# GLU weight gradients: where the attention weights' pieces stand, where the last tile's hh is read from, and when dA's last columns are fetched

## The chip, the cores and the metric

The kernel runs as one program on one core of a Trainium2 chip. The core has five engines that run side by side, each with its own instruction stream in a fixed order: TensorE (PE; its weight loads are listed as PEld), VectorE (DVE), ScalarE (ACT), GpSimd (POOL) and SyncE (SP). Data moves between the device memory (DRAM) and the core's memory (SBUF) by DMA; SP, ACT and POOL issue transfers, each on a queue of its own (q1 is SP's, q10 ACT's, q0 POOL's), and all of them share 16 DMA engines. TensorE writes into PSUM, from which DVE or ACT "evacuates" a result to SBUF.

The metric is the time of one launch in microseconds (us). Three runs of the kernel before gave 3058.02, 3062.4 and 3064.0, median 3062.4.

## The reference, cut to what matters

The program computes the output and all gradients of a two-part layer: a segmented attention with a memory (64 segments of 32 rows, 32 heads of 128) and a gated linear unit (GLU), for 2048 rows of width 512 and a hidden width of F = 1792:

```python
def _B_ref(x, w_gate, w_up, w_down):
    g = jnp.einsum('bsd,df->bsf', x, w_gate)
    u = jnp.einsum('bsd,df->bsf', x, w_up)
    h = _sigmoid(g) * u
    return jnp.einsum('bsf,fd->bsd', h, w_down)
...
x = x + ga * _A_ref(h, A_mem0, A_Wq, A_Wk, A_Wv, A_Wo, A_seg_len)
h = _layernorm(x, axis=-1) * (1 + cb) + sb
x = x + gb * _B_ref(h, B_w_gate, B_w_up, B_w_down)
```

The change lies in the backward pass of the GLU. With h2 the GLU's input rows, hh = sigmoid(g) * u, db the gradient at the GLU's output, and dg and du the gradients at g and u, the three weight gradients are sums over all 2048 rows:

- dW_down = hh^T db (1792 x 512, output 9),
- dW_gate = h2^T dg and dW_up = h2^T du (512 x 1792 each, outputs 7 and 8).

## The kernel before

The program runs in phases. Phase 2 is the attention forward, phase 3 the GLU forward and backward with its weight gradients, phase 4 the attention backward, phase 5 the attention's weight gradients. The change is in phase 3 and in what is prepared there for phase 4.

**The GLU's tiles.** The 2048 rows go through as NT = 16 tiles of 128 rows in a pipeline of seven stages, `s0` to `s6`, one step per iteration `it`, the deepest stage first (`run_pipeline`, L1373). `s2` makes g and u with w_gate and w_up and, in a late part, hh (L1213), which POOL stores to HHROWS (L1214). `s3` makes du and dg (L1232 to L1238); SP turns hh around with a transposing DMA (L1225). `s4` multiplies by w_down (L1247) and turns du and dg around, duT (L1250) and dgT (L1251). `s5` makes the gradient at the GLU's input from duT and dgT (L1272). `s6` sums over rows (L1315), transposes da, the gradient for the attention's output (L1319), and SP stores it to DAOT (L1323). hh, du, dg and the rest live in the pool `sbp`; hh has two buffers.

**W_down's gradient.** Once the last tile has left `s2`, the space of w_gate and w_up (`Wk`) is free. `dbr` (all 2048 rows of db, 2 MB) is loaded there by ACT (L1355, at it = NT + 1) and `hr_0` (all 16 tiles of hh's first 384 columns) by SP (`load_hr(0)`, L1339, at it = NT + 2). hh's other columns come in groups `hr_1` to `hr_4` of 384 columns (the last has 256) into a ring of two places in `Wv`. `wd_chunk(fc)` (L1341 to L1347) makes 128 rows of dW_down: 16 products, one per tile, summed in one PSUM bank, then an evacuation, by ACT and DVE in turns, and a store by POOL. Chunks 0 to 2 (out of hr_0) run inside the pipeline's last steps; chunks 3 to 13 follow in the block with the pools `p3g_o` and `p3g_ps`.

**W_gate's and W_up's gradients.** After that come 2 x NCH = 8 column chunks (4 for dg, 4 for du) of CH = 448 columns, each with DC = 4 results of 128 rows, each result again 16 products (L1427). dg's or du's chunk of columns is loaded by ACT as `xr` (`load_xr`, L1403, 1792 KB) into the same ring of two places in `Wv`, two chunks ahead, and h2 as `h2r` (L1415, 2 MB). The first, `load_xr(0)`, is issued after W_down's chunk 11, when hr_3 has been read.

**The attention weights' pieces.** Phase 4 needs the attention's four weight matrices transposed (WoT, WvT, WkT, WqT). This is cut into 32 pieces (`p4_weights_setup_pieces`, L1468 on): each loads 512 KB by SP into one of three places (`stage0`, `stage1` and a part of `Wv`; L1488 and L1502), runs 16 transposes on TensorE (L1493 and L1506) into two PSUM banks, and has four evacuations by DVE and ACT. `emit_setup()` (L1395) spreads them over the 19 steps of the block, 11 chunks of dW_down and 8 column chunks.

**dA's last columns.** Phase 4 begins with the last four segments. `get_db(15)` (L1464) has SP load the last tile of DAOT (`daq`, L1459) and POOL copy from it (`dyb`, L1466). It is called after W_down's chunk 4.

The order of instructions on each engine is made when the program is built: a scheduler places what the source emits, by readiness, and `pin` fixes parts of it. `evac` is a helper, so evacuations have its lines (L61 for ACT, L63 for DVE).

Of the kernel before, what the change touches and what calls it, by code (L numbers as in the profile page):

```python
# [40 lines left out]
class K:  # L41
# [1035 lines left out]
    def phase3(self):  # L1077
        nc, tc, cfg, io = self.nc, self.tc, self.cfg, self.io
        D, DC, F, FC, NT, T = cfg.D, cfg.DC, cfg.F, cfg.FC, cfg.NT, cfg.T
        CH = 448  # L1080
        NCH = F // CH
# [5 lines left out]
        with ExitStack() as ctx:  # L1087
# [16 lines left out]
            def mm():  # L1104
                return psM.tile([128, 512], F32, name="mm", tag="m")
# [88 lines left out]
            def s2(j, st):  # L1194
                r0, r1 = j * 128, (j + 1) * 128
                hdT = st["hdT"]
                sg = sbp.tile([128, F], BF16, name="sg", bufs=2)
                u = sbp.tile([128, F], BF16, name="u", bufs=1)
                hh = sbp.tile([128, F], BF16, name="hh", bufs=2)
                umh = sbp.tile([128, F], BF16, name="umh", bufs=1)  # L1200
                for ch in range(NCH):
                    sl = slice(ch * CH, (ch + 1) * CH)
                    gp = mm()
                    for c in range(DC):
                        nc.tensor.matmul(gp[:, 0:CH], lhsT=hdT[:, c, :], rhs=w_gate[:, c, sl], start=(c == 0), stop=(c == DC - 1))
                    nc.scalar.activation(sg[:, sl], gp[:, 0:CH], AF.Sigmoid)
                    up = mm()
                    for c in range(DC):
                        nc.tensor.matmul(up[:, 0:CH], lhsT=hdT[:, c, :], rhs=w_up[:, c, sl], start=(c == 0), stop=(c == DC - 1))
                    self.evac("act", u[:, sl], up[:, 0:CH])  # L1210

                def out():
                    nc.vector.tensor_tensor(hh[:], sg[:], u[:], op=ALU.mult)  # L1213
                    nc.gpsimd.dma_start(self.HHROWS[r0:r1, :], hh[:])  # L1214
                    nc.vector.tensor_tensor(umh[:], u[:], hh[:], op=ALU.subtract)

                late.append(out)
                st.update(sg=sg, hh=hh, umh=umh)
                return st

            def s3(j, st):
# [107 lines left out]
            dbr = self.flat(self.Wk, 0, NT * D).rearrange("p (j d) -> p j d", j=NT)  # L1329
            hr_0 = self.flat(self.Wk, NT * D, NT * 384).rearrange("p (j f) -> p j f", j=NT)  # L1330
            hrs = {0: hr_0}
# [3 lines left out]
            kk = [0]  # L1335

            def load_hr(g):
                w = min(384, F - 384 * g)
                (nc.sync if g < 2 else nc.scalar).dma_start(hrs[g][:, :, 0:w], self.HHROWS[:, 384 * g:384 * g + w].rearrange("(j p) f -> p j f", p=128))  # L1339

            def wd_chunk(fc, ps, ot):  # L1341
                for j in range(NT):
                    nc.tensor.matmul(ps[:], lhsT=hrs[fc // 3][:, j, (fc % 3) * 128:(fc % 3) * 128 + 128], rhs=dbr[:, j, :],
                                     start=(j == 0), stop=(j == NT - 1))
                self.evac("act" if kk[0] % 2 == 0 else "dve", ot[:], ps[:])
                kk[0] += 1
                nc.gpsimd.dma_start(io["out_9"][fc * 128:(fc + 1) * 128, :], ot[:])  # L1347

            def after(it):
                for f in turns.pop(it, []):  # L1350
                    f()
                if it == 2:
                    self.pin(i0, [ET.PE, ET.Activation])
                if it == NT + 1:
                    nc.scalar.dma_start(dbr, self.DBROWS[:, :].rearrange("(j p) d -> p j d", p=128))  # L1355
                elif it == NT + 2:
                    load_hr(0)
                elif NT + 3 <= it < NT + 6:
                    if it == NT + 3:
                        load_hr(1)  # L1360
                    wd_chunk(it - NT - 3, mm(), sbp.tile([128, D], BF16, name="ot2", tag="db", bufs=2))
# [4 lines left out]
            def after(it):  # L1366
# [3 lines left out]
                if it >= 5:  # L1370
                    later(it)

            self.run_pipeline(NT, [s0, s1, s2, s3, s4, s5, s6], deepest_first=True, after=after)  # L1373
            self.pin(i0, [ET.DVE])
            self.pin_behind(i0, self.pinned, [ET.PE, ET.DVE, ET.Activation, ET.Pool, ET.SP])
# [8 lines left out]
        with ExitStack() as ctx:  # L1384
            op_ = ctx.enter_context(tc.tile_pool(name="p3g_o", bufs=2, reuse_waits="tile"))
            psG = ctx.enter_context(tc.tile_pool(name="p3g_ps", bufs=4, space=PSUM, reuse_waits="tile"))
            setup_pieces = self.p4_weights_setup_pieces(ctx)
            n_chunks = 2 * NCH + FC - 3
            n_setup, done = len(setup_pieces), [0]

            def emit_setup():
                done[0] += 1
                while setup_pieces and (n_setup - len(setup_pieces)) * n_chunks < done[0] * n_setup:
                    setup_pieces.pop(0)()
            h2r = self.flat(self.Wk, NT * D, NT * D).rearrange("p (j d) -> p j d", j=NT)  # L1395
            load_hr(2)
            xrs = []

            def load_xr(i):
                if i < 2 * NCH:  # L1400
                    rows, ch = ((self.DGROWS, self.DUROWS)[i // NCH], i % NCH)
                    t = ring[i % 2].rearrange("p (j f) -> p j f", j=NT)
                    nc.scalar.dma_start(t, rows[:, ch * CH:(ch + 1) * CH].rearrange("(j p) f -> p j f", p=128))  # L1403
                    xrs.append(t)

            for fc in range(3, FC):
                wd_chunk(fc, psG.tile([128, D], F32, name="gps2", tag="g"), op_.tile([128, D], BF16, name="ot2", tag="o"))
                if fc == 4:
                    self.get_db(cfg.NS // 4 - 1)
                if fc == 5:  # L1410
                    load_hr(3)
                elif fc == 8:
                    load_hr(4)
                elif fc == 9:
                    nc.scalar.dma_start(h2r, self.H2ROWS[:, :].rearrange("(j p) d -> p j d", p=128))  # L1415
                elif fc == 11:
                    load_xr(0)
                emit_setup()
            load_xr(1)
            k = kk[0]  # L1420
            for (rows, outw) in ((self.DGROWS, io["out_7"]), (self.DUROWS, io["out_8"])):
                for ch in range(NCH):
                    xr = xrs.pop(0)
                    for c in range(DC):
                        ps = psG.tile([128, CH], F32, name="gps", tag="g")
                        for j in range(NT):
                            nc.tensor.matmul(ps[:], lhsT=h2r[:, j, c * 128:(c + 1) * 128], rhs=xr[:, j, :],  # L1427
                                             start=(j == 0), stop=(j == NT - 1))
                        ot = op_.tile([128, CH], BF16, name="ot", tag="o")
                        self.evac("act" if k % 2 == 0 else "dve", ot[:], ps[:])  # L1430
                        k += 1
                        nc.gpsimd.dma_start(outw[c * 128:(c + 1) * 128, ch * CH:(ch + 1) * CH], ot[:])
                    load_xr(NCH * (outw is io["out_8"]) + ch + 2)
                    emit_setup()
            while setup_pieces:
                setup_pieces.pop(0)()
        self.wvk_ctx.close()
# [852 lines left out]
```

## Time and profile before

| | us |
|---|---|
| profiled execution | 3064.78 |
| its span | 3063.0 |
| median of the three timed runs | 3062.4 |
| mean granted TensorE clock | 0.991 |
| last product of the GLU's tiles before W_down's chunk 0 (L1247) ends | about 1295.4 |
| W_down's chunk 0 starts | 1299.63 |
| W_down's chunk 3 starts | 1319.27 |
| W_gate's first product starts | 1391.62 |
| last product of W_up ends | about 1503.6 |
| phase 4's first product with dOst (L1742) starts | 1519.57 |

Times inside the execution count from the start of the span. The profile lists, for each engine, its instructions with start and duration; a bracket after a row says how long the engine was idle before it and what it then waited for. A row of several like instructions gives the start of the first and the duration of all of them. A view of stretches gives, for each stretch, the busy time of the engines, the clock that TensorE was granted (1.00 is full) and the share and rate of the DMA engines.

### The profile page before, as it was taken

The page shows a single profiled execution, that of the slowest core. Times are in us where ns is not written, and L with a number is a line of the kernel's source. Part 1 is how long each engine was busy: PE and PEld are TensorE (multiplying, and loading weights), DVE is VectorE, ACT ScalarE, POOL GpSimd, SP SyncE. Part 2 cuts the span into 40 slices and gives each one's busy share as a digit, 9 for nine tenths or more (in the row PEclk, how much of TensorE's full clock was granted, in tenths as well). Part 3 has the DMA queues.
Part 4 walks back from the last instruction along what each step waited for, and adds up shares of the span by engine and source line. Part 5 has one row for each costly group of instructions (what it writes and reads, how often), then busy time and mean ns, then how long its engine had stood idle before and what let it go on. Part 6 is the DMA issues. An engine that isn't in the chain of part 4 may idle for free. (4 is left out here: it accounts for less than half of the span.)

```text
span 3063.0 us, 106593 instructions
## 1 busy us (share of the span) xinstructions
PE 2975.5 (97%) x44297; PEld 1859.8 (61%) x44297; DVE 1605.9 (52%) x3744; ACT 1288.2 (42%) x3182; POOL 1220.6 (40%) x2645
## 2 busy tenths in 40 slices
PE   6999999999998999989899999999999999999999
PEld 3666666666665544445567777777777754445454
DVE  5566566656656788732255555555555632322230
ACT  2555565555554533321255555555555520101011
POOL 2555555555554222211344444444444422333321
PEclk8999999999999999999999999999999999999999
DMA  9888888888888899987499999999999997666574
GB/s 307 217 219 209 216 220 205 219 215 210 217 215 265 199 230 229 239 254 246 155 248 248 245 246 243 247 246 253 248 239 248 246 284 265 214 193 220 182 247 140
DMA packets 838567, 703.54 MB, mean 230 GB/s; under 512 B 538722, under 2 KB 711042, under 8 KB 837188
## 3 DMA queue, kind: packets, MB, share of 16 engines
q1 hardware_dynamic: 712916, 486.69, 64.3%
q0 software_dynamic: 54512, 148.63, 15.3%
q10 hardware_dynamic: 70656, 61.41, 6.4%
q8 instruction: 348, 5.70, 0.8%
q14 instruction: 135, 1.11, 0.1%
HBM read 295.19 MB, written 276.35 MB: 187 GB/s over the span
## 5 line engine op out<-in xcount | busy, mean ns | idle before, releaser
L2080 PE MATMUL gps<-rows,hrows 128*128 128x512 bf16 (+2 forms) x2160 | 417.5, 355 | 0.0
L2080 PEld LDWEIGHTS <-hrows 128*128 128x128 bf16 x2160 | 211.3, 98 | 204.5
L63 DVE CAST ot<-gps 128x512 bf16<-128x512 f32 (+3 forms) x76 | 48.2, 634 | 294.7 <-PE gps L2080 208.4
L1786 POOL COPY dOst<-RAd 96x512 bf16<-96x512 bf16 x128 | 75.1, 611 | 307.6 <-DVE RAd L63 307.3
L61 ACT ACTIVATE ot<-gps 128x512 bf16<-128x512 f32 (+3 forms) x75 | 41.3, 551 | 359.9 <-PE gps L2080 214.7
L658 PE MATMUL pass_ps<-Wv,hT 128*32 128x512 bf16 (+2 forms) x2304 | 188.2, 357 | 0.0
L2084 POOL DMA_DIRECT2D out_dram<-ot x108 | 81.4, 753 | 260.3 <-DVE ot L63 132.7
L1034 POOL TENSOR_TENSOR Pst<-Pst,rden 120x1408 bf16<-120x1408 bf16 x63 | 159.8, 2536 | 56.7 <-issue 35.3
L255 PEld LDWEIGHTS <-hT 128*32 128x32 bf16 x4096 | 125.1, 97 | 94.2 <-DMA Wq<-in_A_Wq_dram 4.6
L61 ACT ACTIVATE dVT<-g_ps 128x480 bf16<-128x480 f32 (+1 forms) x192 | 104.7, 545 | 97.8 <-PE g_ps L1742 97.4
L63 DVE CAST Vst<-pass_ps 96x512 bf16<-96x512 f32 x128 | 87.3, 682 | 106.4 <-ACT RBv L61 101.3
L215 PE MATMUL dh_ps<-WvT,dVT 128*32 128x512 bf16 x2048 | 134.3, 382 | 0.1
L2094 PE MATMUL gps5o<-WoT,rows 128*128 128x512 bf16 x592 | 128.4, 379 | 1.8 <-DMA rows<-OSR 1.8
L255 PE MATMUL pass_ps<-Wq,hT 128*32 128x512 bf16 x2048 | 125.6, 383 | 4.5 <-DMA Wq<-in_A_Wq_dram 4.5
L223 PE MATMUL at_ps<-Wo,OT 128*32 128x256 bf16 x4096 | 124.6, 274 | 2.8 <-DMA Wo<-in_A_Wo_dram 2.4
L658 PE MATMUL pass_ps<-Wv,hb 128*32 128x512 bf16 (+2 forms) x636 | 127.2, 345 | 0.0
L255 PE MATMUL pass_ps<-Wk,hT 128*32 128x512 bf16 x2048 | 124.8, 381 | 1.8 <-POOL hT L547 1.1
L255 PE MATMUL pass_ps<-WoT,dyT 128*32 128x256 bf16 (+1 forms) x3072 | 122.7, 308 | 0.9 <-ACT dyT L1860 0.9
L223 PE MATMUL dhq_ps<-WqT,dQT 128*32 128x256 bf16 x4096 | 122.9, 273 | 0.0
L793 POOL DMA_DIRECT2D Vst<-RBv x192 | 99.2, 522 | 58.6 <-ACT ET L840 38.3
L215 PE MATMUL dh_ps<-WkT,dKT 128*32 128x512 bf16 x2048 | 122.3, 380 | 0.0
L223 PEld LDWEIGHTS <-dQT 128*32 128x32 bf16 x4096 | 109.8, 97 | 15.6
(448 smaller groups left out, 7007.5 us busy)
## 6 DMA issues: line engine op xcount, KB each, us to landing
OSR<-Ost SPq DMA_DIRECT2D x64, 352.0 KB
OT<-OT SPq DMA_DIRECT2D x64, 352.0 KB
VT<-VTr SPq DMA_DIRECT2D x64, 352.0 KB
PS<-Pst SPq DMA_DIRECT2D x64, 352.0 KB
OT_l<-OT SPq DMA_DIRECT2D x64, 352.0 KB
Pst_l<-PS SPq DMA_DIRECT2D x64, 352.0 KB
VT_l<-VT SPq DMA_DIRECT2D x64, 352.0 KB
DVR<-rows_x POOLq DMA_DIRECT2D x64, 352.0 KB, 6.2
```

The source lines that it names most:

```text
L61: return nc.scalar.activation(out, in_, AF.Copy)
L63: return nc.vector.tensor_copy(out, in_)
L215: self.nc.tensor.matmul(ps[32 * j:32 * j + 32, :], lhsT=lhsT, rhs=w, start=(n < 4), stop=(n >= total - 4), tile_position=(0, 32 * j))
L223: nc.tensor.matmul(ps[32 * j:32 * j + 32, :], lhsT=x[k], rhs=w[k][:, 256 * d:256 * d + 256], start=(n == 0), stop=(n == total - 1), tile_p ...
L255: self.nc.tensor.matmul(ps[32 * j:32 * j + 32, :], lhsT=lhs(c), rhs=rhs, start=(c == 0), stop=(c == DC - 1), tile_position=(0, 32 * j))
L658: nc.tensor.matmul(ps[32 * j:32 * j + 32, o * E:(o + n) * E], lhsT=lhsT, rhs=wc[:, 3 * a + hl:3 * (a + n - 1) + hl + 1:3, :], start=(c == ...
L793: nc.gpsimd.dma_start(Vst[96 + 8 * j:104 + 8 * j, :], rb[32 * j + o:32 * j + o + 8, :])
L1034: nc.gpsimd.tensor_tensor(Pst[0:120, :, :], Pst[0:120, :, :], rden[:, :].unsqueeze(2).to_broadcast([120, G, 128]), op=ALU.mult)
L1786: nc.gpsimd.tensor_copy(dOst[0:96, 512 * hf:512 * hf + 512], RAd[0:96, 512 * hf:512 * hf + 512])
L2080: nc.tensor.matmul(ps[:, 0:ng * E], lhsT=hrows[:, tp_, c * 128:(c + 1) * 128], rhs=rows[:, tp_, 0:ng * E], start=(tp_ == 0), stop=(tp_ == ...
L2084: nc.gpsimd.dma_start(outw[c * 128:(c + 1) * 128, h0:h0 + 3 * (ng - 1) + 1:3, :], ot[:, 0:ng * E].rearrange("p (h e) -> p h e", e=E))
L2094: nc.tensor.matmul(pss[gg][:], lhsT=src[0][:, src[1], gg * E:(gg + 1) * E], rhs=dyrows[:, tp_, :], start=(tp_ == order[0]), stop=(tp_ == o ...
```

## The change

Four things are edited, all in phase 3:

1. `load_hr(0)` is emitted one step earlier, at it = NT + 1 and ahead of dbr, is issued by ACT instead of SP, and loads 15 tiles instead of 16.
2. For the chunks 0 to 2, the product of the last tile reads hh from that tile's own buffer in SBUF (`last_hh`), not from hr_0.
3. `emit_setup(n)` counts units: 3 for each W_down chunk and 8 for each of the 32 gate and up products (289 in all), and is called after each of those products instead of after each column chunk.
4. `get_db(15)` is called after W_gate's first column chunk instead of after W_down's chunk 4. `load_xr` keeps its place, after a chunk's last product.

```diff
                 st.update(sg=sg, hh=hh, umh=umh)
+                if j == NT - 1:
+                    last_hh.append(hh)
                 return st
...
             def load_hr(g):
-                w = min(384, F - 384 * g)
-                (nc.sync if g < 2 else nc.scalar).dma_start(hrs[g][:, :, 0:w], self.HHROWS[:, 384 * g:384 * g + w].rearrange("(j p) f -> p j f", p=128))
+                w, n = min(384, F - 384 * g), NT if g else NT - 1
+                (nc.sync if g == 1 else nc.scalar).dma_start(
+                    hrs[g][:, 0:n, 0:w], self.HHROWS[0:128 * n, 384 * g:384 * g + w].rearrange("(j p) f -> p j f", p=128))
+
+            last_hh = []
 
             def wd_chunk(fc, ps, ot):
                 for j in range(NT):
-                    nc.tensor.matmul(ps[:], lhsT=hrs[fc // 3][:, j, (fc % 3) * 128:(fc % 3) * 128 + 128], rhs=dbr[:, j, :],
+                    rows = last_hh[0][:, 0:384] if fc < 3 and j == NT - 1 else hrs[fc // 3][:, j, :]
+                    nc.tensor.matmul(ps[:], lhsT=rows[:, (fc % 3) * 128:(fc % 3) * 128 + 128], rhs=dbr[:, j, :],
                                      start=(j == 0), stop=(j == NT - 1))
...
                 if it == NT + 1:
+                    load_hr(0)
                     nc.scalar.dma_start(dbr, self.DBROWS[:, :].rearrange("(j p) d -> p j d", p=128))
-                elif it == NT + 2:
-                    load_hr(0)
                 elif NT + 3 <= it < NT + 6:
...
-            n_chunks = 2 * NCH + FC - 3
+            units = 3 * (FC - 3) + 8 * 2 * NCH * DC
             n_setup, done = len(setup_pieces), [0]
 
-            def emit_setup():
-                done[0] += 1
-                while setup_pieces and (n_setup - len(setup_pieces)) * n_chunks < done[0] * n_setup:
+            def emit_setup(n):
+                done[0] += n
+                while setup_pieces and (n_setup - len(setup_pieces)) * units < done[0] * n_setup:
                     setup_pieces.pop(0)()
...
                 wd_chunk(fc, psG.tile([128, D], F32, name="gps2", tag="g"), op_.tile([128, D], BF16, name="ot2", tag="o"))
-                if fc == 4:
-                    self.get_db(cfg.NS // 4 - 1)
                 if fc == 5:
                     load_hr(3)
...
                     load_xr(0)
-                emit_setup()
+                emit_setup(3)
             load_xr(1)
...
                         nc.gpsimd.dma_start(outw[c * 128:(c + 1) * 128, ch * CH:(ch + 1) * CH], ot[:])
-                    load_xr(NCH * (outw is io["out_8"]) + ch + 2)
-                    emit_setup()
+                        if c == DC - 1:
+                            load_xr(NCH * (outw is io["out_8"]) + ch + 2)
+                        emit_setup(8)
+                    if outw is io["out_7"] and ch == 0:
+                        self.get_db(cfg.NS // 4 - 1)
```

## The prediction

> **What bounds the kernel now.** I read the page's parts 1 and 4 first. TensorE is busy for 97% of the span and holds most of the chain that ended last, so a microsecond in which it idles, or runs at a reduced clock, is a microsecond of the result. The waits of TensorE alone, over the stretch the change touches (1290 to 1520 us), say which microseconds those are:
>
> ```profile
> PE 2975.5 (97%) x44297; PEld 1859.8 (61%) x44297; DVE 1605.9 (52%) x3744; ACT 1288.2 (42%) x3182; POOL 1220.6 (40%) x2645
> ```
> ```profile
> PE g_ps L1742 <- DMA dOst<-RBd: 8.1, 1, 8.1
> PE wtp L1493 <- DMA Wv<-in_A_Wv_dram: 4.3, 1, 4.3
> PE mm L1343 <- DMA Wk<-HHROWS: 4.0, 1, 4.0
> PE wtp L1506 <- DVE WoT L63: 3.9, 1, 3.9
> PE wtp L1506 <- DMA stage<-in_A_Wo_dram: 1.6, 1, 1.6
> PE gps L1427 <- DMA Wv<-DGROWS: 1.1, 1, 1.1
> PE wtp L1493 <- DMA stage<-in_A_Wk_dram: 0.9, 1, 0.9
> ```
>
> Each row: who waited, for whom, us in total, times, longest. Six of these lie between the GLU's last tile and the end of the weight-gradient products. A long wait costs twice, as the stretches show (us, PE busy, ..., PEclk, DMA share, GB/s):
>
> ```profile
> 1300.00:1302.00 2.00, 2.00 (x6) 0.73 (x5) 0.03 (x1) 0.00 (x0) 0.53 (x1) 0.50 1.18 349
> 1336.00:1340.00 4.00, 2.42 (x28) 1.55 (x26) 1.18 (x3) 0.94 (x2) 1.05 (x4) 1.00 1.11 349
> 1363.40:1368.00 4.60, 4.60 (x26) 2.59 (x27) 1.28 (x3) 0.60 (x1) 0.00 (x0) 0.63 0.22 66
> 1395.00:1503.00 108.00, 108.00 (x713) 60.70 (x711) 23.20 (x50) 19.43 (x34) 16.74 (x31) 1.00 0.61 202
> ```
>
> After the 4.0 us wait the granted clock is 0.50, after the 4.3 us wait 0.63; the 1.6 us wait leaves it at 1.00. From 1395 us on, where some 12 pieces lie among the gate and up products, TensorE is never idle and DMA has a share of 0.61 only. So the waits sit where loads crowd, and pieces cost nothing beyond their own work where they do not.
>
> **The change part by part.** Unit prices come from TensorE's order of time (start, us):
>
> ```profile
> 1185.64 3.19 PE L1247 MATMUL mm<-Wv,hhT 128*128 128x512 bf16 x14
> 1188.66 3.19 PE L1232 MATMUL mm<-w_downT,hdT 128*128 128x448 bf16 x16
> ...
> 1422.71 11.32 PE L1427 MATMUL gps<-Wv,Wk 128*128 128x448 bf16 x59
> ```
>
> 14 products of 512 columns from one start to the next take 3.02 us, 0.216 each, so a W_down chunk of 16 takes 3.46. Products of 448 columns take 0.19, so a gate or up product (16 of them) 3.03. A piece (16 transposes) costs TensorE 1.0 us: from 1448.06 to 1450.58 there are one piece and 8 products of 0.19.
>
> (1) hr_0 without its last tile, on ACT's queue behind dbr. Before, it is issued by SP at 1288.83 and releases TensorE at 1299.63, 4.03 us late:
>
> ```profile
> 1288.83 0.44 SPq L1339 DMA_DIRECT2D Wk<-HHROWS  x1
> 1299.63 5.09 PE L1343 MATMUL mm<-Wk 128*128 128x512 bf16 x16 [4.03 <-DMA Wk<-HHROWS]
> 1319.27 3.62 PE L1343 MATMUL gps<-Wk,Wv 128*128 128x512 bf16 x16
> ```
>
> In the built order of the changed program it stands right behind dbr (issued at 1272.62) and w_up's last evacuation, at about 1273.7: 22 us before its use. The wait goes, and with it the half clock (5.09 against 3.62 us for the same 16 products): 4.03 + 1.47 = -5.5 us. Three products read hh in SBUF instead of hr_0: same shape, 0.
>
> What is late next: 1.44 MB more stream on ACT's queue from 1279 us, beside the last tiles' DMA transposes on SP's queue. Nothing shows that pair, but dbr does. Between 1273 and 1281 us the DMA view lists only
>
> ```profile
> q10 hardware_dynamic: 1718, 1.76, 71.3%
> q0 software_dynamic: 109, 0.67, 26.3%
> ```
>
> q10 is ACT's queue; SP's, q1, has nothing there, although duT was issued at 1276.84 (and took 4.03 us to issue; 1.51 in the tile before). So a transpose behind ACT's stream starts some 4 us late. Work queued from 1273.7: dbr and hr_0, 2.10 + 1.47 MB at 349 GB/s (the stretch 1300 to 1302 above), 10.2 us; HHROWS 0.46 MB, 1.3; duT 1.7 (0.46 MB at 271 GB/s, the rate of 1284 to 1286): done at 1286.9, where TensorE wants duT at 1285.71; with landing 1.6 us late. Bounds: 0 (no wait there now) and 5.5 (it takes the place of what it removes, clock and all). I take +1.6; dgT and hhT, 3 and 6 us later, then have their margin back, and at 1.6 us the clock stays up.
>
> A rule to weigh here: the Trainium skill, "DMA: Bandwidth & Descriptors", section "Queues, rings and completion order", says that each DMA engine goes round its queues packet by packet, so that duT would share from its issue on and be in time, and this term would be 0. The 4 us without a byte on q1 speak against it, and the measurement decides.
>
> (2) Pieces by products. Before, 32 pieces over 19 steps put 19 of them among the 11 W_down chunks of phase "p3g"; after, 3 x 11 of 289 units leave 4 there and 28 among the 32 gate and up products. The work is moved, not removed: 15 us leave one part and enter the other. The waits at 1338 (1.6), 1363 (4.3), 1389 (0.9) and at W_gate's start (1.1) hang on loads that then no longer crowd: -7.9 us. The clock: 1363.38 to 1368.54 hold 16 transposes and 12 products, 3.5 us of work in 5.2, so -1.7; 1389.86 to 1394.92 likewise 2.2 us of work and 1.1 of wait in 5.1, so -1.7. Together -11.3; at worst 0, if every one comes back.
>
> New waits: W_down now runs at 3.46 us a chunk, so loads have less time. hr_3 has 3 chunks and a piece, 11.4 us; xr_0 only two chunks and a piece, 7.9 us. Nearest rows: xr_0 before, issued at 1378.92, released TensorE at 1391.62, 12.7 us with 2 MB of pieces' loads around it; 1792 KB at 377 GB/s would be 4.9. So 0 to 4.8 us (and 1.7 of clock). With one piece's load beside it I take 9 us: 1.1 of wait and 0.4 of clock, +1.5. In the gate part a chunk takes 4 x 3.03 + 3.5 x 1.0 = 15.6 us and moves 1.84 MB of xr, 1.84 of pieces and 0.46 of results, 265 GB/s of some 331 (202 GB/s at a share of 0.61): covered. Without that cover, rival B.
>
> (3) The wait of 3.9 us at 1328 stays: DVE holds WoT until daT's store has landed, and store and queue order around it are unchanged: 0 (bounds: -6.4 with its clock, 0).
>
> (4) dA's last columns (get_db): in the built order POOL's dyb copy still stands between the fourth and fifth W_down store, where it waits 11.4 us for daq. No effect, 0; no TensorE row waits on those stores.
>
> (5) The end. Phase 4 starts through POOL:
>
> ```profile
> 1505.47 1.27 POOL L1556 MEMSET dS<- 128x1408 bf16 x1 [0.32 <-PE wtp L1493]
> 1513.86 1.57 POOL L1672 DMA_DIRECT2D dOst<-RBd  x3
> 1519.57 0.56 PE L1742 MATMUL g_ps<-Pst_l,dOst 128*128 128x120 bf16 x4 [8.05 <-DMA dOst<-RBd]
> ```
>
> Now the last piece comes behind the last product (which ends near 1503.6) and the memset at +1.9 us; in the built order it comes before it, the memset follows the product, and one result store (0.54) slips behind it: dOst's DMA 1.25 us earlier, less 0.9 us for the piece that is now ahead: -0.35 (bounds -1.3, +1).
>
> Sum: -5.5 + 1.6 - 11.3 + 1.5 - 0.35 = -14 us. On the profiled execution, span 3063.0 and 3064.78 in all, that gives 3050.7; that execution stands 2.4 above the median 3062.4, from which the same sum gives 3048.4. I forecast **3049**. Its own range is 3043 to 3056: term (1) or the new wait of (2) at its worse bound adds 4 to 5, and the shown times scatter by 3.
>
> **The rivals.** A: the W_down part becomes bound by loads. From the third chunk of mm() to the first gate product, 8.1 MB of hr_2, h2r, hr_3, hr_4 and xr_0, 2.1 of pieces and 1.4 of results come in; at 263 GB/s (the DMA view of 1320 to 1390) 44 us, against 42 of products and pieces plus 6 for the stall of (3). For it: 0.83 DMA share in that part now. Against: the same loads had 70 us there along with 10 MB of pieces. If hr_3, hr_4 and xr_0 each come 2 us later than I reckon: 3049 + 6 = 3055.
>
> B, slower than before: the gate part becomes bound by xr. Its load for chunk n + 2 leaves when chunk n ends and has one chunk, 15.6 us; it decides once issue to landing passes that. Seen so far: up to 12.7 us. Should 28 pieces' loads on SP's queue stretch it to 18, each of 7 chunks waits 2.5 us and pays 1.7 of clock: 29 us, 3049 + 29 = 3078. Against it: 265 of 331 GB/s.
>
> C: hr_0's stream holds back duT, dgT and hhT in turn, so that one wait replaces another: +5.5 instead of +1.6, 3053.
>
> D: the stall of (3) goes too, because less is queued at that time: 3049 - 6 = 3043.
>
> E: the change doesn't do what it says, the waits return elsewhere piece by piece: 3062, no change.
>
> **How the numbers follow.** Forecast 58%, A 12%, C 11%, D 8%, E 5%, B 6%. Under 0.2% (6.1 us, 3056.3 to 3068.5) a measurement of this kernel can't be told from no change. Faster: forecast, C, D and most of A, 0.86; same: E and the rest of A, 0.08; slower: B, 0.06. The range 3041 to 3059 takes in A, C and D with the run-to-run 3 us of the shown times.
>
> **What would show it.** No wait of L1343's successor on HHROWS at the first chunk, and its 16 products in 3.6 us at clock 1.00; a wait of 1 to 2 us on duT near 1286; pieces as 16 transposes per gate product with no wait on stage or Wv; a wait of about 1 us on DGROWS at W_gate's start; the 3.9 us before WoT unchanged; phase 4's first product of scores near 1505 to 1507. I am wrong if gate products wait for DGROWS or DUROWS more than once, or if the wait on duT passes 4 us and the clock falls there.

## The result, and the profile after

| | kernel before | changed kernel |
|---|---|---|
| median, runs of the first comparison (7 each), us | 3058.02 (3054.06 to 3064.0) | 3049.13 (3046.22 to 3052.53) |
| ratio to before, 95% interval | | 0.9966 (0.9956 to 0.9975) |
| second comparison: medians, us | 3060.99 (11 runs) | 3052.72 (7 runs) |
| its ratio | | 0.9968 (0.9958 to 0.9979) |
| profiled execution, us; span; clock | 3064.78; 3063.0; 0.991 | 3048.13; 3046.3; 0.993 |

The change makes the kernel faster by 0.34%, which is 10.4 us of 3061 (7.7 to 13.5 by the interval); the quotient of the two first medians alone would be 0.9971. The two profiled executions differ by 16.65 us, more than the runs do; where that surplus sits is shown below.

TensorE's waits in the changed kernel, 1270 to 1520 us (who waited, for whom: us in total, times, longest):

```profile
PE g_ps L1748 <- DMA dOst<-RBd: 6.8, 1, 6.8
PE mm L1274 <- DMA duT<-du: 3.4, 1, 3.4
PE wtp L1512 <- DVE WoT L63: 2.6, 1, 2.6
PE gps L1430 <- DMA Wv<-DGROWS: 1.1, 1, 1.1
PE gps L1349 <- ACT ot L61: 0.7, 1, 0.7
...
PE mm L1249 <- DMA hhT<-hh: 0.4, 1, 0.4
```

The rows on HHROWS (4.0 before), on the pieces' part of Wv (4.3) and on stage (1.6 and 0.9) are gone. New are duT, ot and hhT, 4.5 us together. The order of time on TensorE (start, us) shows how fast the products go behind the waits on duT and DGROWS, and the stretch behind the first of them (us, busy by engine, then clock, DMA share, GB/s) shows what is left of idle time:

```profile
1290.59 3.20 PE L1274 MATMUL mm<-Wq,duT 128*128 128x512 bf16 x13 [3.36 <-DMA duT<-du]
...
1301.14 3.40 PE L1349 MATMUL mm<-Wk 128*128 128x512 bf16 x14
...
1366.31 3.20 PE L1430 MATMUL gps<-Wv,Wk 128*128 128x448 bf16 x16 [1.05 <-DMA Wv<-DGROWS]
```
```profile
1295.40:1488.00 192.60, 186.63 (x1298) 104.50 (x1304) 59.23 (x133) 41.89 (x73) 29.42 (x58) 1.00 0.79 250
```

Behind the wait on duT the granted clock is 1.00 (1290.59 to 1293.60 us), and 16 products of 448 columns take the 3.20 us that they take elsewhere: neither wait cost any clock. Over 192.6 us TensorE idles for 6.0, at a clock of 1.00.

**Where the time went, stage by stage.** The distances between the starts of five rows of TensorE: the last tile's products with w_downT (a), W_down's chunk 3 (b), W_gate's first product (c), phase 4's first product with dyb (d) and its first product of dhq_ps (f). Two executions of each kernel, us:

| stretch | before | before, again | after | after, again |
|---|---|---|---|---|
| a to b: end of the tiles, chunks 0 to 2 | 36.6 | 37.5 | 36.2 | 36.3 |
| b to c: W_down's chunks 3 to 13 | 72.4 | 67.4 | 46.1 | 46.5 |
| c to d: W_gate, W_up | 112.4 | 111.0 | 124.6 | 124.5 |
| d to f: start of phase 4 | 26.1 | 24.2 | 23.1 | 23.1 |
| a to f | 247.4 | 240.2 | 229.9 | 230.3 |
| row a starts at | 1282.7 | 1287.0 | 1284.0 | 1291.1 |

The first pair gives 17.5 us, the second 9.9, and only the second agrees with the timed ratio. The execution profiled before the prediction was a poor sample of exactly the stretch in question: its waits on stage and the pieces' Wv came to 6.8 us, against 3.9 in the second execution of the same program. The last row shows that all the work ahead of the change, which is the same in both kernels, scatters by 8 us as well. So one pair of profiles tells where time goes, and the timed runs tell how much.

### The profile page after: what moved, and what is told of

Same layout as the page of the kernel before. It is cut to its first block, busy times and chain, and to the rows that moved or that the text cites. A ratio compares the mean times of both kernels' runs of the same rounds, so it can differ in the third digit from the quotient of the medians.

```text
span 3046.3 us, 106520 instructions
## 1 busy us (share of the span) xinstructions
PE 2965.3 (97%) x44223; PEld 1858.1 (61%) x44297; DVE 1604.1 (53%) x3744; ACT 1286.8 (42%) x3182; POOL 1220.3 (40%) x2645
## 4 chain that ended last, share of the span: by engine, by line
PE 44%; issue 4%; DMA 1%; POOL 1%; SPq 0%; DVE 0%; ACT 0%; ACTq 0%; POOLq 0%
PE gps L2086 9%; PE dh_ps L215 8%; PE g_ps L1748 6%; PE pass_ps L255 5%; PE gps5o L2100 4%; PE dhq_ps L223 4%; PE dh_tps L215 3%; PE dp_ps L1725 2%; PE tps L1658 2%; PE dp_ps L1733 1%; PE turn_ps L1612 1%; PE dh_ft L323 1%; POOL out_dram L2090 1%; DMA rows<-DVR 1%; DMA rows<-OSR 0%
```

## The experiments

All ratios are to the kernel before, run on the same chip in the same rounds, with a 95% interval.

**1. Each part alone.** The pieces' edit alone (hr_0 and get_db as before):

```diff
-            n_chunks = 2 * NCH + FC - 3
+            units = 3 * (FC - 3) + 8 * 2 * NCH * DC
...
-                emit_setup()
+                emit_setup(3)
...
-                    emit_setup()
+                        emit_setup(8)
```

> Only the spreading of the pieces; hr_0 as before (SP, 16 tiles, after hhT). Theory 1 (the gain comes from the pieces, and hr_0's part is given back at duT): 9 to 13 us below the kernel before; TensorE's wait of about 4 us on HHROWS at the first W_down chunk stays, no wait over 0.5 us on duT; from W_down's chunk 3 to W_gate's first product about 46 us as in the changed kernel (72.4 before). Theory 2 (hr_0's part brings the 4 to 5 us it was given, and duT's wait in the changed kernel is one execution's accident): 5 to 8 us below.

Measured: 0.9979 (0.9968 to 0.9989), median 3052.45. The same kernel once more in a later set:

> The pieces' edit alone once more, on a chip with other variants. The first time it gave 0.9979 [0.9968, 0.9989], the whole change 0.9966 and 0.9968. Theory 1 (hr_0's edit is worth nothing, as its own run at 1.0005 shows): 0.9965 to 0.998. Rival (the two edits help each other): 0.998 to 0.999, and the whole change stays ahead by 0.1% or more.

Measured: 0.9971 (0.9960 to 0.9983), median 3052.73. The waits are those of theory 1, but the price is not: the two ratios stand for 6.4 and 8.9 us, below its 9 to 13, and from b to c the kernel takes 50.0 and 47.7 us, not 46. hr_0's edit alone (early on ACT, 15 tiles, `last_hh`; pieces and get_db as before):

> Only hr_0 early on ACT's queue with 15 tiles, and the last tile's hh from SBUF; pieces as before. Theory 1: within 2 us of the kernel before; no wait on HHROWS, but 3 to 4 us on duT; from the last w_down product of tile 15 to W_down's chunk 3 36 to 37 us, as before and after. Theory 2: 4 to 5 us below the kernel before, no wait on duT over 1 us, and that stretch 31 to 32 us.

Measured: 1.0005 (0.9996 to 1.0015), median 3061.67. And the kernel before once more, as a yardstick for how the waits recur:

> The kernel before, unchanged, for a second profile. If the waits are a matter of the order, the seven rows of TensorE's waits come back within 1 us each, and the time equals the kernel before within its scatter. If they are a matter of one execution, the rows on HHROWS, stage and Wv differ by several us, and that is where the 10 us between the seven shown times of before come from.

Measured: 1.0003 (0.9993 to 1.0012), median 3059.96. TensorE's waits of the three, first the pieces alone:

```profile
PE g_ps L1743 <- DMA dOst<-RBd: 6.9, 1, 6.9
PE wtp L1507 <- DVE WoT L63: 3.7, 1, 3.7
PE mm L1343 <- DMA Wk<-HHROWS: 3.4, 1, 3.4
PE gps L1427 <- DMA Wv<-DGROWS: 1.3, 1, 1.3
```

then hr_0 alone:

```profile
PE wtp L1511 <- DMA stage<-in_A_Wo_dram: 3.9, 1, 3.9
PE mm L1274 <- DMA duT<-du: 3.1, 1, 3.1
PE wtp L1498 <- DMA Wv<-in_A_Wv_dram: 2.9, 1, 2.9
PE wtp L1511 <- DVE WoT L63: 2.5, 1, 2.5
```

and the kernel before, second execution:

```profile
PE wtp L1506 <- DVE WoT L63: 4.3, 1, 4.3
PE mm L1343 <- DMA Wk<-HHROWS: 3.8, 1, 3.8
PE wtp L1493 <- DMA Wv<-in_A_Wv_dram: 2.4, 1, 2.4
PE wtp L1506 <- DMA stage<-in_A_Wo_dram: 1.5, 1, 1.5
```

Each edit removes the rows that it was meant to. The pieces' edit carries the gain: 6 to 9 us of the 10. hr_0's edit swaps HHROWS for duT and gains nothing that these runs can see. Of the two readings expected for the kernel before, each is half right: the long waits come back in its second execution, but Wv's is 1.9 us shorter, and the short ones on stage (0.9, in_A_Wk) and DGROWS (1.1) are not there at all. The changed kernel itself, again, beside the variants of experiments 3, 5 and 6:

> The changed kernel as it is, beside the variants of the same set. Waits fixed by the built order should recur within about 1 us of the first profile: duT 3.4, WoT 2.6, dOst 6.8, none on HHROWS, stage or the pieces' part of Wv. Ratio to the kernel before 0.996 to 0.997 if the first comparison (0.9966) is typical; a theory that the first gain was luck of one chip would see 0.999 to 1.000.

Measured: 0.9968 (0.9958 to 0.9979), with waits of 6.8 on dOst, 3.0 on duT, 2.8 on WoT, 1.4 on DGROWS, all within 0.4 us of the first execution. The intervals of the pieces alone and of the whole change overlap, so no help of one edit to the other is shown. get_db was not run apart: with its call put back, the built program has the same order on TensorE, ACT, POOL and SP.

**2. hr_0 a little later.** If hr_0's stream holds up duT, let it start behind duT.

```diff
                 if it == NT + 1:
-                    load_hr(0)
                     nc.scalar.dma_start(dbr, self.DBROWS[:, :].rearrange("(j p) d -> p j d", p=128))
+                elif it == NT + 2:
+                    load_hr(0)
```

> The changed kernel with hr_0's load one step later on ACT's queue: behind tile 13's dh2b evacuation, about 6 us later, when duT's transpose has its descriptors out. Theory 1: the wait on duT goes (under 1 us), hr_0 is still in time for the first chunk (issue near 1282, use near 1295, 8 to 11 us to land), at most 1 to 2 us of wait on dgT or hhT: 2 to 4 us below the changed kernel, 12 to 16 below the one before. Theory 2: no difference to the changed kernel beyond 1 us.

Measured: 0.9991 (0.9980 to 1.0002), median 3057.17: most of the gain is lost.

```profile
PE mm L1274 <- DMA dgT<-dg: 6.0, 1, 6.0
PE mm L1274 <- DMA duT<-du: 3.0, 1, 3.0
```

My expectation fell. duT waits as before, and dgT, which waited for nothing in the changed kernel, now stops TensorE for 6 us, after which its first products show 0.61 us each. Of the last tile's transposes, the stream now holds up the second as well. This is rival C of the prediction, made real by a later start.

**3. How hr_0 slows duT: fewer bytes, the same number of packets.** hr_0 is split. Its first 128 columns come early on ACT, the other 256 by SP, where the kernel before issued hr_0.

```diff
+            def load_hr0(eng, lo, hi):
+                n = NT if lo else NT - 1
+                eng.dma_start(hrs[0][:, 0:n, lo:hi], self.HHROWS[0:128 * n, lo:hi].rearrange("(j p) f -> p j f", p=128))
...
-                    rows = last_hh[0][:, 0:384] if fc < 3 and j == NT - 1 else hrs[fc // 3][:, j, :]
+                    rows = last_hh[0][:, 0:384] if fc == 0 and j == NT - 1 else hrs[fc // 3][:, j, :]
...
-                    load_hr(0)
+                    load_hr0(nc.scalar, 0, 128)
...
+                elif it == NT + 2:
+                    load_hr0(nc.sync, 128, 384)
```

> hr_0 split: its first 128 columns (0.49 MB, 15 tiles) early on ACT's queue behind dbr as in the change, its other 256 columns (16 tiles) by SP where the kernel before had hr_0. Theory 1 (duT is late because of the bytes queued on ACT's queue ahead of it): 0.98 MB less at some 349 GB/s is 2.8 us, so the wait on duT falls from 3.4 to about 0.6 us; chunk 0 has its columns, and the second part lands by about 1297 to 1300 as nothing else is behind it, so no wait on HHROWS or up to 1 us at chunk 1; 2 to 4 us below the changed kernel, ratio 0.995 to 0.9965. Rival (the number of transfers or of descriptors decides, not the bytes: rows of 256 bytes go as slowly as rows of 768): the wait on duT stays at 2.5 to 3.5 us. Second rival: the second part holds back the last tiles' transposes as the late hr_0 did, with a new wait on duT, dgT or hhT of the last tile of 3 us or more.

Measured: 0.9963 (0.9950 to 0.9977), median 3049.56; the changed kernel beside it has 0.9968, so that a gain in time isn't shown. The wait on duT is 1.5 us, between the two theories (0.6 and 2.5 to 3.5). The traffic by queue while duT moves tells why (packets, MB, share of 16 engines; q1 is SP's, q10 ACT's). The changed kernel, 1285 to 1288 us:

```profile
q10 hardware_dynamic: 1007, 0.78, 77.2%
q1 hardware_dynamic: 999, 0.26, 37.7%
```

hr_0 split, the same 3 us:

```profile
q10 hardware_dynamic: 1652, 0.42, 64.8%
q1 hardware_dynamic: 1643, 0.41, 63.9%
```

the pieces alone, where hr_0 is not yet there, 1283 to 1286 us:

```profile
q1 hardware_dynamic: 3045, 0.77, 124.7%
q10 hardware_dynamic: 42, 0.03, 3.4%
```

In these stretches the two queues move the same number of packets: 1007 and 999, 1652 and 1643. A packet of the transposes is a row of 256 bytes, one of hr_0's whole rows has 768, one of the split's 256. So, by estimate, duT's 0.46 MB, some 1790 packets, take 1790 / 333 per us = 5.4 us beside whole rows, 1790 / 548 = 3.3 beside short rows and 1790 / 1015 = 1.8 alone. The steps between these, 2.1 and 1.5 us, are near those of the wait: 2.9 to 3.6 us in the six executions with the whole rows early, 1.5 with the split, none without. Equal shares are no rule for every stretch, though: in the kernel of experiment 2, ACT's queue moves 609 packets between 1289 and 1291 us and SP's 387, and in the kernel before, between 1355 and 1357 us, ACT's moves 1095 and SP's 3, although SP had issued a load at 1354.25.

**4. Why the pieces no longer wait.** The prediction put the waits down to loads that crowd in W_down's part. Two kernels take this apart. One has one piece after each W_down chunk, 11 there (19 before, 4 after the change), and 21 spread over the products:

```diff
-            units = 3 * (FC - 3) + 8 * 2 * NCH * DC
+            units = 32 * (FC - 3) + 21 * 2 * NCH * DC
...
-                emit_setup(3)
+                emit_setup(32)
...
-                        emit_setup(8)
+                        emit_setup(21)
```

> The changed kernel with one piece after each W_down chunk (11 there, against 19 before and 4 after the change) and 21 spread over the 32 products. Theory 1 (crowding by volume: pieces' loads against hr, h2r and xr in W_down's part): between the two, stage and Wv waits in W_down of 1.5 to 4 us in sum, against 4 to 7 before and none after the change; 1 to 5 us above the changed kernel, ratio 0.997 to 0.998. Rival (bursts of two between chunks made the waits, not the volume): no stage or Wv wait at one piece per chunk, ratio 0.9965 or lower, and DGROWS' wait at W_gate's start gone because 7 us more of pieces cover xr_0.

Measured: 0.9972 (0.9962 to 0.9983), median 3050.43. The ratio fits theory 1, the waits fit the rival. TensorE has no row on stage or on the pieces' Wv at all:

```profile
PE g_ps L1748 <- DMA dOst<-RBd: 7.0, 1, 7.0
PE mm L1274 <- DMA duT<-du: 2.9, 1, 2.9
PE wtp L1512 <- DVE WoT L63: 2.9, 1, 2.9
PE mm L1249 <- DMA hhT<-hh: 1.3, 1, 1.3
```

Nor is the rate lower there. From b to c, the stretches of the kernel before and of this one read

```profile
1319.27:1391.62 72.35, 60.37 (x458) 34.55 (x457) 23.45 (x53) 17.10 (x29) 8.94 (x20) 0.93 0.83 264
```
```profile
1323.20:1376.53 53.33, 49.64 (x337) 27.33 (x344) 15.02 (x34) 10.63 (x19) 7.54 (x17) 0.97 0.90 280
```

that is, 264 GB/s with waits, 280 GB/s without. So the rate over the whole part does not make the waits. What the spacing of the pieces does is seen on one buffer. The kernel before, SP's issue of a load and TensorE's first transpose from it:

```profile
1354.25 0.37 SPq L1488 DMA_DIRECT2D Wv<-in_A_Wv_dram  x1
```
```profile
1363.38 0.40 PE L1493 MATMUL wtp<-ident,Wv 128*128 128x128 bf16 x4 [4.32 <-DMA Wv<-in_A_Wv_dram]
```

one piece per chunk:

```profile
1351.73 0.37 SPq L1508 DMA_DIRECT2D Wv<-in_A_Wo_dram  x1
```
```profile
1362.31 0.61 PE L1512 MATMUL wtp<-ident,Wv 128*128 128x128 bf16 x8
```

With two pieces per chunk TensorE was back at the buffer 4.8 us after the load's issue (9.13 less the wait of 4.32), and the load took 9.1. With one piece per chunk there were 10.6 us, and nothing waited. Three buffers carry three pieces; what has to hold is that the time from a load's issue to its use is longer than the load takes. The traffic beside these two loads is not the same, however:

```profile
1354.25:1363.38 9.13, 4.78 (x46) 2.94 (x44) 2.54 (x6) 2.28 (x4) 0.54 (x1) 1.00 0.91 299
```
```profile
1351.73:1362.31 10.58, 10.48 (x72) 5.77 (x73) 3.05 (x7) 2.28 (x4) 1.08 (x2) 1.00 0.82 256
```

It is 299 GB/s in the kernel before and 256 with one piece per chunk. Pieces in pairs thus leave their loads less time and also crowd them, and the kernel with one piece per chunk has fewer pieces there, too (11 for 19). Which of these counts for most was not taken apart: no kernel has 19 evenly spaced pieces in this part, or 11 in pairs.

The other kernel keeps the change's weights, 4 and 28, but calls the gate part's pieces in bursts after each column chunk:

```diff
-                        emit_setup(8)
+                        if c == DC - 1:
+                            emit_setup(8 * DC)
```

> The changed kernel with the same weights (4 pieces in W_down, 28 in the gate and up part), but the gate part's pieces called once per column chunk, in bursts of 3 or 4, as the kernel before called them. Theory 1 (what matters is that loads crowd in W_down's part and not in the gate part): a burst of 3 finds its three buffers loaded during the 12 us of products before it, only a fourth piece waits, as its load starts when the first has been turned; 0.5 to 2 us at four chunks, so 2 to 8 us above the changed kernel, ratio 0.998 at the middle. Rival (bursts themselves are the price, wherever they are): 3 us and a fallen clock at most chunks, +15 us and more, ratio 1.001 and above. Second rival (place alone decides, spreading is worth nothing): no stage or Wv wait, ratio 0.9965.

Measured: 0.9981 (0.9973 to 0.9990), median 3056.47. The size is that of theory 1, the place only in small part:

```profile
PE g_ps L1749 <- DMA dOst<-RBd: 8.0, 1, 8.0
...
PE wtp L1513 <- DMA Wv<-in_A_Wo_dram: 1.1, 1, 1.1
...
PE wtp L1500 <- DMA stage<-in_A_Wk_dram: 0.4, 1, 0.4
```

Only two of the fourth pieces wait (1.1 us at 1392, 0.4 at 1455; 12 us of products lie between bursts). But the last burst comes behind W_up's last product, so that three pieces stand in the start of phase 4, where their work is bare: d to f takes 29.6 us, against 23.1. By the two ratios (0.9981 and 0.9968), spreading by products is worth some 4 us beyond the weights, but their intervals overlap.

**5. All 32 pieces among the products, none in W_down.**

```diff
-            units = 3 * (FC - 3) + 8 * 2 * NCH * DC
+            units = 8 * 2 * NCH * DC
...
-                emit_setup(3)
```

> All 32 pieces stand among the 32 gate and up products, one each, none in W_down. Theory 1 (a piece costs TensorE nothing beyond its 16 transposes as long as its load has room, and the gate part has it; the WoT wait hangs on the last daT store, which has long landed by the gate part): the wait on WoT (2.6) goes, no stage or Wv wait appears, the wait on DGROWS at W_gate's start grows from 1.1 to 2 to 5 us because 4 us of pieces no longer cover xr_0's load; net -1 to +2 us against the changed kernel, ratio about 0.9965. Rival (rivals A and B of the prediction: loads crowd as soon as one part holds them all): stage or Wv waits in the gate part, 1 us or more each at several of 32 pieces, +10 us and more, ratio 1.000 and above. Second rival: the wait on WoT is not tied to the daT store and comes back at the first piece in the gate part.

Measured: 0.9964 (0.9952 to 0.9977), median 3049.97. No row on stage, the pieces' Wv or WoT is left. DGROWS is as short as in the changed kernel, against the 2 to 5 us expected, and HHROWS's, which is new, is short too:

```profile
PE gps L1429 <- DMA Wv<-DGROWS: 1.2, 1, 1.2
PE gps L1349 <- DMA Wv<-HHROWS: 1.1, 1, 1.1
```

From b to c 40.7 us, from c to d 127.7: the WoT wait (2.6) is gone, HHROWS takes 1.1 back, and four more pieces cost the gate part 3.1. What b to d gains in this profile (168.4 us against 170.6) a to b loses (38.6 against 36.2), where duT is waited for for 3.63 us and the clock falls; 0.9964 against 0.9968 beside it shows no difference. One piece of 0.5 MB per product of 3.03 us still finds room in the gate part, so rival B (that part bound by loads) has not even begun. The wait on WoT goes with pieces that come early: in the changed kernel DVE itself waits 2.7 us there for daT's store to DAOT before it evacuates WoT, and here it has no such wait.

**6. A version that beats both.** Experiments 3 and 5 together, and phase 4's first three small transfers of dOst issued by ACT, not by POOL, where they stand behind six zeroings (dO_tails is given the issuing engine as an argument):

```diff
-            dO_tails(NS - 1)
+            dO_tails(NS - 1, nc.scalar)
```

> The changed kernel with the pieces all among gate and up products, hr_0 split, and phase 4's first three small transfers of dOst issued by ACT instead of POOL (where they stand behind six memsets). Theory 1: wait on dOst falls from 6.8 to 1 to 3 us, since RBd is ready some 5 us before POOL's issue at 1499.95; with the two other edits as in their own runs, 5 to 10 us below the changed kernel, ratio 0.993 to 0.995. Rival: another input (Qst, Kst or Pst loads, or dOT) ends last in the tail and the wait is renamed: under 2 us gained there, ratio 0.9955 and above.

Measured: 0.9939 (0.9926 to 0.9951), median 3043.61; the changed kernel in the same set has 0.9968 (0.9958 to 0.9979).

```profile
PE g_ps L1753 <- POOL dOst L1797: 2.8, 1, 2.8
PE gps L1353 <- DMA Wv<-HHROWS: 1.7, 1, 1.7
PE mm L1274 <- DMA duT<-du: 1.5, 1, 1.5
PE gps L1435 <- DMA Wv<-DGROWS: 1.0, 1, 1.0
```

The wait on dOst falls from 6.8 to 2.8 and changes its releaser from a DMA to POOL's copies. Then two of POOL's zeroings, of Qst and Kst, were given to DVE:

```diff
-                        nc.gpsimd.memset(t[:], 0.0)
+                        (nc.vector if name in ("Qst", "Kst") else nc.gpsimd).memset(t[:], 0.0)
```

> The version with everything (pieces among products only, hr_0 split, dOst's transfers on ACT), with the zeroing of Qst and Kst on DVE instead of POOL. There the wait on dOst was 2.8 us, for POOL's copies behind six zeroings of 1.2 us each; two fewer take 2.4 us off POOL's queue. Theory 1: that wait falls to 0.4 to 1 us, 2 us below that version's 3043.6, ratio 0.993 to 0.9935. Rival: DVE, which also evacuates RBd and btd there, or the loads of Qst and Kst now ahead of Pst in SP's queue, takes its place: 0 to +3 us, ratio 0.994 to 0.995.

Measured: 0.9952 (0.9940 to 0.9964), median 3045.96. By the waits the rival was right: dOst is waited for through its DMA again, longer than in the version above. The two times come from different chips, and their intervals overlap, so a loss in time isn't shown.

```profile
PE g_ps L1753 <- DMA dOst<-RBd: 5.6, 1, 5.6
```

SP's queue shows what came in between. In this kernel the loads of Qst and Kst go out before ACT issues dOst's three transfers at 1492.76:

```profile
1491.36 0.35 SPq L1668 DMA_DIRECT2D Qst<-QST  x1
1492.08 0.33 SPq L1668 DMA_DIRECT2D Kst<-KST  x1
```

In the version above they go out at 1495.45 and 1496.67, after those transfers (1492.42), since POOL had not yet zeroed their places. That 0.66 MB now rides beside 48 KB that are wanted first is read from this order; it was not tested by itself.

## Why the prediction was right, and where it was not

The time (3049 against 3049.13) and the side were right. The way there has one reading that fell and two sizes that were off and cancelled: the sum of -14 us was some 4 too large, and the median that it started from, 3062.4 over three runs, lay 1.4 to 4.4 us above what more runs of the same kernel gave (3058.0, 3060.9, 3061.0). That the forecast fell within 1 us of the time is luck; the second comparison gave 3052.72 for the same kernel.

- **Term (1), hr_0: -5.5 + 1.6.** The removal was right, 4.03 us and the clock behind it. The step that failed is "I take +1.6; dgT and hhT, 3 and 6 us later, then have their margin back". duT's wait was 3.36 us, within the bounds, and 0.45 on hhT and 0.73 on the evacuation ahead of chunk 3 came on top, so a to b shrank by 0.4 and 1.2 us in the two pairs, not by 3.9; alone the edit gave 1.0005. Rival C had the mechanism and nearly the price, and it was given 11%.
- **The rule weighed there.** The Trainium skill, "DMA: Bandwidth & Descriptors", section "Queues, rings and completion order", has the engines go round their queues packet by packet. I set it aside because q1 had no bytes for 4 us after duT's issue. The runs show both. The silence is there without hr_0 too: with the pieces alone, duT is issued at 1276.34 and q1 moves its mass of packets from 1283 on. So duT did not share from its issue on, as I had read the rule; no row shows whether its queue already held work then. Once it moves, the packets stand one to one (experiment 3). What would have come nearer is to count packets, not bytes: beside 768-byte packets a transpose's 256 bytes get a quarter of the rate.
- **Term (2), the pieces: -11.3 and +1.5.** The waits went, all of them, and with them the fallen clock; DGROWS came with 1.1 and 1.4 us at full clock, as reckoned. The size was taken from one execution with 6.8 us on stage and Wv. b to d shrank by 14.1 us against that execution and by 7.5 against the second; the edit alone, timed, gave 6 to 9 us, with the tail in it. "Loads that then no longer crowd" was too coarse a reason: experiment 4 shows 280 GB/s over W_down's part without a wait. What the waits go with is pieces in pairs, which leave a load less time before its use and crowd it for some us.
- **Term (3), WoT: 0.** Its wait was 2.6 and 2.8 us after, 3.9 and 4.3 before, but 2.5 and 3.7 with the pieces alone and 2.5 with hr_0 alone. It stays, with that scatter; rival D did not happen. The scatter costs clock as well, which the term has only in its bound: behind the wait of 3.7 us (the pieces alone) the next 43 products take 12.19 us, behind 2.6 (the changed kernel) 9.66. So some of what b to d shrank by belongs here and not to the pieces.
- **Term (4), get_db: 0.** The built order is the same with and without it (experiment 1).
- **Term (5), the tail: -0.35.** d to f shrank by 1.1 us against the second execution before (3.0 against the first), and with the pieces alone as well, 23.3 and 23.6 us. The lower bound, -1.3, was nearer than the value taken, but the kernels of experiments 2 and 3, with the same order there, took 24.6 and 25.0 us against the changed kernel's 23.1, so that such pairs don't give its size.
- **Rivals A and B.** Neither the W_down part nor the gate part became bound by loads, not even with all 32 pieces in the latter.

## What to carry to other kernels

Before a wait is put down to crowded transfers, compare the rate in the stretch that waits with one that doesn't, and do it for the few us of the load itself: over the whole part the rates here hid that difference (264 and 280 GB/s against 299 and 256). Then look at how soon each buffer is wanted again after its load was issued. A load moved earlier is charged to whatever shares the time, and where two queues alternate by packets, as hr_0 and duT did here, a transfer of 256-byte packets beside one of 768-byte packets gets a quarter of the rate. And size a gain on more than one execution: the long waits on DMA kept their place here, but not their length.

## What the runs showed of the hardware that was not expected

- **A DMA transpose that meets ACT's stream starts late, whatever is queued behind.** Its issue takes 4.79 us in the changed kernel (1.5 in undisturbed tiles), and q1 moves almost nothing until some 6 us after the issue at 1278.19 (1 to 2 us after the one at 1259.38, undisturbed). Its mass of packets begins as dbr's last ones go, near 1285 us here and near 1283 with the pieces alone; whether it waits for these was not tested:

```profile
1278.19 4.79 SPq L1252 DMA_TRANSPOSE duT<-du  x1
1283.14 6.60 SPq L1253 DMA_TRANSPOSE dgT<-dg  x1
```

- **Where the clock falls.** Waits of 3.36 us (above) and 3.38 (the pieces alone, on HHROWS) left it at 1.00. One of 3.86 (the same kernel again) did not; neither, with the bursts, did one of 3.11, where the first product behind it takes 0.61 us, nor, with hr_0 alone, one of 2.85 on Wv, with a clock of 0.50 behind it (1363.5 to 1366 us):

```profile
1290.04 0.61 PE L1274 MATMUL mm<-Wq,duT 128*128 128x512 bf16 x1 [3.11 <-DMA duT<-du]
```

The Trainium skill, "TensorE: Matmul & The Clock Gate", section "Part 1: The HAM clock gate", gives an idle window of about 3.4 us. The runs agree on the size, and they show no sharp edge: between 2.85 and 3.4 us it went either way.
